# Attention and two feed-forward blocks: scores of the first two pairs made in 32-column strips instead of spread through SBUF

## The chip, the cores and the metric

The kernel runs on one core of one Trainium2 chip. Five engines work from queues of their own and meet at semaphores: PE (matrix products, with its weight loads, PEld), DVE and ACT (vector and activation work), POOL and SP. DMA transfers are issued from the queues of SP, ACT and POOL. The metric is the device time of one execution in microseconds (us), lower is better.

## What is computed

Inputs are q, k, v of shape (2, 12, 448, 64): two batches, twelve heads, 448 rows, 64 columns. Attention mixes the heads twice, before and after softmax:

```
scores = scale * q @ k.T                             # b h i j
scores = einsum('bhij,hg->bgij', scores, w_pre)      # mix heads
attn   = exp(scores - max) / (sum + 1e-9)            # over j
attn   = einsum('bhij,hg->bgij', attn, w_post)       # mix heads
x      = attn @ v                                    # to (896, 768)
x      = ((x @ w_a) * (x @ w_b)) @ w_out             # d_ff 1536
out    = relu(x @ w_in) ** 2 @ w_out2                # d_ff 2048
```

## The kernel before

All matrix products of the two feed-forward blocks follow the attention; they are not touched. Attention goes through the 448 rows of a batch in four tiles of 120, 120, 120 and 88 rows. A tile consists of blocks of ten rows, and two blocks make a **pair**, the unit of the pipeline: six pairs in a full tile, 23 in a batch. `NC` = 6 chunks hold two heads each.

Scores of a tile come from `qk` (L169): for each chunk two matmuls, one per head, on the two halves of the array's rows, with the 120 query rows as output rows and the 448 key columns as moving operand. For the first two tiles they are plain float32; later tiles use a high and a low part of each operand (three products). `qk_copy` (L188) brings the scores to SBUF, the even head by ACT and the odd one by DVE.

The mixing of heads wants another order: for one block, 120 partitions that hold twelve heads times ten rows. So `spread` (L196) sends each head's scores by DMA into `G`, in which partition `13*row + head` holds a score row and the second index counts the blocks. There are two of these, G[0] for tiles zero and two, G[1] for tiles one and three. `premix` (L223) then does the first mixing of a pair: four 64x64 matmuls from G with `wpre_sb`, in the four quadrants of the array, into two banks with the tag `T`.

`softmax` (L625) takes the minima (DVE, L239) and the exponentials (ACT, L246), `weights2` (L252) scales the second mixing's weights by the sums, `post` (L268) does the second mixing (32 small matmul records per pair), `evac` (L285) copies it out. After a tile's pairs, `av` (L301) multiplies with v in three blocks. The main loop (L637) goes through **slots**, one per pair: first mixing of the next pair, second mixing of this one, softmax of the next, and then what a table `mid` gives to the slot (score chunks of a later tile, loads, casts, splits), and `end` (the values). Each engine runs its instructions in the order in which the program writes them.

The start has an order of its own. SP loads the six key chunks, ACT's queue three parts of the first queries, the mixing weights and the queries of tile one. Twelve chunks of scores, six of tile zero and six of tile one, run back to back; tile zero goes to G in three portions (`GS`: blocks 0-1, 2-5 and 6-11), tile one in one. Warming matmuls (`busy`, L339) stand before, between and behind. Portions three of tile zero, the queries of tile two, the spreads of tile one and the load of v follow in `spread_rest` (L369), all behind one another on SP and POOL.

Of the kernel before, what the change touches and what calls it, by code (L numbers as in the profile page):

```python
# [20 lines left out]
KG = 5  # L21
# [43 lines left out]
def attention_moe_kernel(  # L65
    ctx: ExitStack,
    tc: tile.TileContext,
    qT: bass.AP,
    kT: bass.AP,
    v: bass.AP,  # L70
    wpre: bass.AP,
# [16 lines left out]
        return ap.bitcast(F32)  # L88


    wpre_sb = const.tile([128, 128], F32, name="wpre_sb")
    wp = const.tile([128, H, KG], F32, name="wp")

    def single(tag, dtype=F32R):
# [29 lines left out]
    qp = {}  # L124
    qq = {}
    vv = {}
    AVp = {}

    def load_q(b, t, engs=(nc.sync,)):
        x = w_p.tile([128, UW], F32, tag="wc", name="q", bufs=2)  # L130
        n = NC * TILE // len(engs)
        for i, eng in enumerate(engs):
            eng.dma_start(out=x[:, i * n:(i + 1) * n], in_=qT[b, t, :, i * n:(i + 1) * n])
        qq[b, t] = x


    def load_k(b, c):
# [30 lines left out]

    def qk(b, t, c, tags=("qk", "qk")):  # L169
        qk_out()  # L170
        n = ROWS[t]
        p = [ps(tag) for tag in tags]
        if b == 0 and t < 2:
            parts = [(qq[b, t], kk[b, c])]
        else:
            (qh, ql), (kh, kl) = qp[b, t], kp[b, c]
            parts = [(qh, kh), (qh, kl), (ql, kh)]
        for i, (x, y) in enumerate(parts):
            for e in range(2):
                o = 64 * e  # L180
                nc.tensor.matmul(  # L181
                    p[e][0:n, 0:S], x[o:o + 64, c * TILE:c * TILE + n], y[o:o + 64, :],
                    start=(i == 0), stop=(i == len(parts) - 1),
                )
        for e in range(2):
            Sps.append((b, t, 2 * c + e, p[e]))

    def qk_copy(t, h, p, s):  # L188
        n = ROWS[t]
        if h % 2:  # L190
            nc.vector.tensor_copy(s[0:n], p[0:n, 0:S])
        else:
            nc.scalar.copy(s[0:n], p[0:n, 0:S])


    def spread(t, h, s, r0, r1, eng=nc.sync):  # L196
        g = G[t % 2]
        n = r1 - r0
        o = r0 * ROW
        last = ROW - 1 if h == H - 1 else ROW  # L200
        eng.dma_start(out=g[h:PK * (last - 1) + h + 1:PK, r0:r1, :], in_=s[o:o + last * n])
        if last < ROW:
            a = place(last, h)
            eng.dma_start(out=g[a:a + 1, r0:r1, :], in_=s[o + last * n:o + ROW * n])


    def qk_out(which=(0, 1)):
        now = [x for x in Sps if x[2] % 2 in which]
        Sps[:] = [x for x in Sps if x[2] % 2 not in which]
        for b, t, h, p in now:  # L210
            n = ROWS[t]
            s = s_p.tile([TILE, S], F32, tag="s", name="s")
            qk_copy(t, h, p, s)
            full = n // ROW
            spread(t, h, s, 0, full)
            rem = (n - full * ROW) // 2
            for f in range(2 if rem else 0):
                o = full * ROW + f * rem
                a = place(f * KG, h)
                nc.sync.dma_start(out=G[t % 2][a:a + PK * (rem - 1) + 1:PK, full, :], in_=s[o:o + rem])  # L220


    def premix(b, m):  # L223
        t, r, n = PAIRS[m]
        p = [ps("T") for _ in range(2)]
        for g in range(n):
# [6 lines left out]
        Tps[b, m] = p  # L233

    def smin(b, m, f):
        if f == 0:
# [93 lines left out]
    nc.gpsimd.memset(G[0][:, GS[0]:GS[1], :], 0.0)  # L330
    nc.vector.memset(G[0][:, GS[1]:GS[2], :], 0.0)
    nc.gpsimd.dma_start(out=wp, in_=wpost)
    nc.gpsimd.memset(G[0][:, GS[2]:GS[3], :], 0.0)
    nc.vector.memset(G[1][:, 0:6, :], 0.0)
    nc.gpsimd.memset(G[1][:, 6:H, :], 0.0)
    nc.vector.tensor_scalar(wpre_sb, wpre_sb, -0.125, None, ALU.mult)


    def busy(n):  # L339
# [7 lines left out]
    v0 = [sb.tile([128, NJ * DM], F32, tag="v", name="v0", bufs=2) for _ in range(2)]  # L347
    stage1 = [v0[h // 6][0:TILE, (h % 6) * S:(h % 6 + 1) * S] for h in range(H)]
    tags0 = (("qk", "qk"), ("T", "T"), ("post", "post"))
    hw = (nc.gpsimd, nc.sync)  # L350
    for c in range(NC):
        qk(0, 0, c, tags0[c % 3])
        while Sps:
            _, t, h, p = Sps.pop(0)
            qk_copy(t, h, p, stage0[h])
            spread(0, h, stage0[h], GS[0], GS[1], hw[h % 2])
    for h in range(H):
        spread(0, h, stage0[h], GS[1], GS[2], hw[h % 2])
    for c in range(NC):
        qk(0, 1, c, tags0[c % 3])  # L360
        while Sps:
            _, t, h, p = Sps.pop(0)
            qk_copy(t, h, p, stage1[h])
    for c in range(3):
        split_k(0, c)
    busy(4)


    def spread_rest():  # L369
        for c in range(3, NC):  # L370
            split_k(0, c)
        for h in range(H):
            spread(0, h, stage0[h], GS[2], GS[3], hw[h % 2])
        load_q(0, 2)
        for h in range(H):
            spread(1, h, stage1[h], 0, ROWS[1] // ROW, hw[h % 2])
        load_v(0)


    tiles = [(b, t) for b in range(B) for t in range(NTL)]  # L380
# [4 lines left out]
    dve_l, mid, end = {}, {}, {}  # L385

    def at(d, slot, *f):
        d.setdefault(max(slot, 0), []).append(f)

    for ti, (b, t) in enumerate(tiles):  # L390
        s0, sp = base[ti], span[ti]
        if ti + 1 < len(tiles):
            nxt = tiles[ti + 1]
            for c in range(NC if ti else 0):
                at(mid, s0 - 3 + c, qk, *nxt, c)
            if ti + 2 < len(tiles):
                if ti:
                    at(mid, s0 - 2, load_q, *tiles[ti + 2])
                at(mid, s0 + 1, split_q, *tiles[ti + 2])
# [301 lines left out]
def _layout(i):  # L701
# [1 line left out]

    f = np.float32
    q, k, v = i["q"], i["k"], i["v"]
    qT = np.zeros((B, NTL, 128, NC, TILE), f)
    for b, t in np.ndindex(B, NTL):
        n = ROWS[t]
        full = n // ROW
        col = []  # L710
        g = GS if b + t == 0 else (0, full)
        for r0, r1 in zip(g, g[1:]):
            p = np.arange((r1 - r0) * ROW)
            col.append(ROW * (r0 + p % (r1 - r0)) + p // (r1 - r0))
        col = np.concatenate(col + [np.arange(full * ROW, n)]) + OFFS[t]
        qT[b, t, :, :, 0:n] = q[b][:, col, :].reshape(NC, 2, n, D).transpose(1, 3, 0, 2).reshape(128, NC, n)
    kT = k.reshape(B, NC, 2, S, D).transpose(0, 1, 2, 4, 3).reshape(B, NC, 128, S)
    vl = v.reshape(B, H, NJ, JP, D).transpose(0, 3, 2, 1, 4).reshape(B, JP, NJ, DM)
    wpre = np.zeros((128, 128), f)
    wpost = np.zeros((128, H, KG), f)  # L720
    for n in range(ROW):
        for g in range(2):
            o = [place_mixed(g, n, h) for h in range(H)]
            wpre[np.ix_([place(n, h) for h in range(H)], o)] = i["w_pre"]
            wpost[o, :, n % KG] = i["w_post"]

    def units(m):
        kk, n = m.shape
# [6 lines left out]
    return {"qT": qT.reshape(B, NTL, 128, NC * TILE), "kT": kT, "v": vl, "wpre": wpre, "wpost": wpost, "w": wall}  # L735


# [18 lines left out]
```

## Time and profile before

| | |
|---|---|
| median of the runs shown | 759.58 us (758.59 to 760.4, three runs) |
| the profiled execution | 753.42 us, of which its span 751.6 |
| PE busy | 730.6 us, 97% |
| DVE, ACT, POOL busy | 485.4, 310.6, 54.0 us |
| mean granted clock of PE | 0.968 of full |
| read from HBM, written | 62.03 MB, 2.75 MB |

Times in the profile start at the span's beginning. Busy is a share of the whole span; a busy PE can still run at half clock, which the row PEclk tells: 1.00 is 2.4 GHz and 0.50 is 1.2 GHz. The chain of waits is followed back from the last instruction: at each step it names what released the work, or the instruction before it on its engine. A name such as `T<-G` gives output and input by the program's names; `L229` is a line of the program. A float32 matmul leaves two records, so four 64x64 matmuls are x8.

### The profile page before, as it was taken

What the parts mean: (1) busy time and instruction counts of PE and PEld (TensorE: products, weight loads), DVE (VectorE), ACT (ScalarE), POOL (GpSimd) and SP (SyncE); (2) the same over time, 40 slices, a digit from 0 to 9 for tenths busy, and PEclk for the clock granted to TensorE, in tenths of its full rate; (3) what the DMA queues carried; (4) which work ended last, traced back from release to release, by engine and by line L of the source; (5) the groups of instructions that cost most, each with busy time, mean ns of one, the idle gap of its engine ahead of it and who ended that gap; (6) DMA issues with size and microseconds to landing.
All of it is one profiled execution on the core that took longest, in us unless ns stands there. A gap on an engine that the chain in (4) does not pass through costs nothing.

```text
span 751.6 us, 13028 instructions
## 1 busy us (share of the span) xinstructions
PE 730.6 (97%) x5301; PEld 622.3 (83%) x5301; DVE 485.4 (65%) x818; ACT 310.6 (41%) x581; POOL 54.0 (7%) x58
## 2 busy tenths in 40 slices
PE   8799989999989999999999999999999999999997
PEld 3567757676757899999999999999999999999997
DVE  6445666577785477666766765666888888655540
ACT  5244564465562433433343332333555555322220
POOL 8500130000220000000000000000000000000000
PEclk9559999999988999999999999999999999999999
DMA  6773443455230032332332233232323323443310
GB/s 179 171 198 110 126 133 120 129 169 165 76 102 34 2 127 92 119 126 85 126 117 95 92 133 112 85 126 85 126 98 112 124 88 126 150 130 130 127 48 26
DMA packets 26969, 84.89 MB, mean 113 GB/s; under 512 B 3634, under 2 KB 16606, under 8 KB 26686
## 3 DMA queue, kind: packets, MB, share of 16 engines
q1 hardware_dynamic: 24910, 80.65, 33.1%
q0 software_dynamic: 1280, 2.62, 1.7%
q8 instruction: 42, 0.69, 0.4%
q10 hardware_dynamic: 720, 0.80, 0.3%
q14 instruction: 17, 0.14, 0.1%
HBM read 62.03 MB, written 2.75 MB: 86 GB/s over the span
## 4 chain that ended last, share of the span: by engine, by line
PE 91%; DMA 4%; DVE 2%; ACT 1%; issue 1%; SPq 1%; DVEq 0%; ACTq 0%
PE post L279 9%; PE T L507 8%; PE T L508 8%; PE T L506 8%; PE qk L506 6%; PE post L508 6%; PE post L507 6%; PE post L506 5%; PE qk L508 5%; PE qk L507 5%; PE T L229 5%; PE qk L181 4%; PE av L310 4%; PE av L506 3%; PE av L507 3%; PE av L508 3%
## 5 line engine op out<-in xcount | busy, mean ns | idle before, releaser
L279 PEld LDWEIGHTS post<-w,e 64*112 64x112 f32 x1440 | 85.7, 194 | 37.0 <-issue 17.3
L459 ACT CAST wh<-wc 128x768 fp32r<-128x768 f32 x68 | 56.8, 835 | 123.4 <-DVE wc L453 109.9
L246 ACT ACTIVATE e<-T,nb 128x448 f32<-128x448 f32 (+1 forms) x92 | 57.4, 629 | 89.7 <-DVE nb L239 89.6
L279 PE MATMUL post<-w,e 64*112 64x60 f32 x1440 | 92.2, 281 | 2.3 <-DVE w L260 2.3
L464 DVE TENSOR_TENSOR wl<-wc,wh 128x768 fp32r<-128x768 f32 x66 | 63.0, 954 | 48.4 <-ACT wh L459 48.4
L507 PE MATMUL T<-m,wh 128*128 128x448 f32 x213 | 77.9, 366 | 0.2 <-DVE m L482 0.2
L506 PE MATMUL T<-m,wh 128*128 128x448 f32 x213 | 77.9, 366 | 0.0
L508 PE MATMUL T<-m,wl 128*128 128x448 f32 x213 | 77.8, 365 | 0.0
L239 DVE TENSOR_REDUCE nb<-T 128x1 f32<-128x448 f32 (+1 forms) x92 | 53.1, 618 | 30.4 <-PE T L229 30.3
L442 DVE SCALAR_TENSOR_TENSOR wa<-wr,wa 128x768 uint32<-128x768 uint32 x68 | 65.2, 958 | 2.3
L453 DVE SCALAR_TENSOR_TENSOR wc<-wc,wa 128x768 uint32<-128x768 uint32 x68 | 65.1, 958 | 2.2
L229 PE MATMUL T<-G,wpre_sb 64*64 64x448 f32 x360 | 54.1, 616 | 8.1 <-DMA G<-x 3.2
L437 ACT ACTIVATE wc<-wr 128x768 f32<-128x768 f32 x68 | 61.4, 903 | 0.0
L449 DVE TENSOR_SCALAR wc<-wc 128x768 f32<-128x768 f32 x68 | 37.7, 554 | 14.7 <-ACT wc L437 14.7
L508 PE MATMUL post<-m,wl 128*128 128x448 f32 x125 | 45.7, 365 | 0.0
L506 PE MATMUL post<-m,wh 128*128 128x448 f32 x125 | 45.6, 365 | 0.0
L507 PE MATMUL post<-m,wh 128*128 128x448 f32 x125 | 45.6, 365 | 0.0
L296 DVE COPY a<-post 112x480 f32<-112x480 f32 x44 | 30.1, 684 | 20.6 <-PE post L279 18.7
L507 PEld LDWEIGHTS T<-m,wh 128*128 128x128 f32 x213 | 40.0, 188 | 3.7 <-DVE m L482 0.5
L506 PEld LDWEIGHTS T<-m,wh 128*128 128x128 f32 x213 | 40.0, 188 | 3.4 <-ACT m L481 0.3
L508 PEld LDWEIGHTS T<-m,wl 128*128 128x128 f32 x213 | 40.0, 188 | 3.1
L506 PE MATMUL qk<-m,wh 128*128 128x448 f32 x116 | 42.4, 365 | 0.0
(160 smaller groups left out, 1441.1 us busy)
## 6 DMA issues: line engine op xcount, KB each, us to landing
wr<-w SPq DMA_DIRECT2D x68, 768.0 KB
G<-s SPq DMA_DIRECT2D x44, 210.0 KB
G<-s SPq DMA_DIRECT2D x22, 140.0 KB
k<-kT SPq DMA_DIRECT2D x12, 224.0 KB
v<-v SPq DMA_DIRECT2D x2, 1344.0 KB
outT<-ta SPq DMA_DIRECT2D x12, 224.0 KB
q<-qT SPq DMA_DIRECT2D x6, 360.0 KB
G<-v POOLq DMA_DIRECT2D x6, 210.0 KB, 11.9
```

Of the source, the lines that this page charges most:

```text
L229: nc.tensor.matmul(p[f][o:o + 64, 0:S], wpre_sb[i:i + 64, o:o + 64], G[t % 2][i:i + 64, r + g, :], start=True, stop=True, skip_group_check ...
L239: nc.vector.tensor_reduce(out=NB[b, m][0:q, f:f + 1], in_=Tps[b, m][f][0:q, 0:S], op=ALU.min, axis=AX.X)
L246: nc.scalar.activation(out=e[0:q], in_=Tps[b, m][f][0:q, 0:S], func=ACTF.Exp, bias=NB[b, m][0:q, f:f + 1], scale=-1.0, accum_out=Z[b, m][0 ...
L279: nc.tensor.matmul(p[g][0:JP, c:c + k], e[o:o + 64, j * JP:(j + 1) * JP], w2[o:o + 64, f, :], start=True, stop=True,)
L437: nc.scalar.activation(out=st["c"], in_=rd(st["high"]), func=ACTF.Abs, scale=HSC)
L442: nc.vector.scalar_tensor_tensor(out=a, in0=st["high"], scalar=0x80000000, in1=a, op0=ALU.bitwise_and, op1=ALU.bitwise_or)
L453: nc.vector.scalar_tensor_tensor(out=cu, in0=cu, scalar=3, in1=st["a"], op0=ALU.logical_shift_left, op1=ALU.bitwise_or)
L459: nc.scalar.copy(st["hi"], st["c"])
L464: eng.tensor_tensor(out=lo, in0=st["c"], in1=rd(st["hi"]), op=ALU.subtract)
L506: nc.tensor.matmul(p[:, 0:S], hi[:, sl], x[0], start=first, stop=False)
L507: nc.tensor.matmul(p[:, 0:S], hi[:, sl], x[1], start=False, stop=False)
L508: nc.tensor.matmul(p[:, 0:S], lo[:, sl], x[0], start=False, stop=last)
```

## The change

The scores of the first two pairs (`ND` = 2: blocks 0 to 3 of tile zero) no longer go through `spread`. A new input `qD` holds their queries so arranged that `direct` makes a block's scores in the mixing's order: for each block two groups of four matmuls over 128 rows with 32 output columns each, in four strips of columns; a strip adds up two chunks, the halves of `qD` that do not belong to a head being zero. One copy per block brings the 128 partitions to SBUF, and `premix` mixes such a block with 128x64 matmuls and a second copy of the mixing weights. The other eight blocks of tile zero are made by `qk` with 80 instead of 120 rows and go to G in one portion. The scores of tile one are no longer made at the start; two of their chunks stand in each of slots 0 to 2, one ahead of the second mixing and one behind it, and their spreads alternate between POOL and SP. The load of the queries of tile two moves to slot 0, key splits to slots 1 to 3, the load of v to slot 2. Warming matmuls remain only at the very start.

```
-GS = (0, 2, 6, 12)
+ND = 2
+R0 = 2 * ND
+ROWS0 = ROWS[0] - R0 * ROW
+CHUNKS = ((0, 1, 3, 4), (1, 2, 4, 5))
...
+    def load_qd(m, tag, bufs, eng):
+        x = w_p.tile([128, UW], F32, tag=tag, name="qd", bufs=bufs)
+        eng.dma_start(out=x[:, 0:512], in_=qD[m])
+        qd[m] = x
...
-            s = s_p.tile([TILE, S], F32, tag="s", name="s")
-            qk_copy(t, h, p, s)
+            first = b == 0 and t == 1
+            s = stage1(h) if first else s_p.tile([128, S], F32, tag="s", name="s")
+            qk_copy(n, h, p, s)
             full = n // ROW
-            spread(t, h, s, 0, full)
+            spread(t, h, s, 0, full, hw[h % 2] if first else nc.sync)
...
+    def direct(m):
+        for g in range(2):
+            p = ps("T" if g else "av")
+            for i in range(2):
+                for j in range(4):
+                    o = ((g * 2 + i) * 4 + j) * 32
+                    nc.tensor.matmul(
+                        p[32 * j:32 * j + 32, 0:S], qd[m][:, o:o + 32], kk[0, CHUNKS[i][j]],
+                        start=(i == 0), stop=(i == 1), skip_group_check=True,
+                    )
+            x = s_p.tile([128, S], F32, tag="s", name="s")
+            if g:
+                nc.scalar.copy(x, p[:, 0:S])
+            else:
+                nc.vector.tensor_copy(x, p[:, 0:S])
+            Sd[m, g] = x
...
     def premix(b, m):
...
+        if b == 0 and m < ND:
+            for f in range(2):
+                for g in range(2):
+                    nc.tensor.matmul(
+                        p[f][64 * g:64 * g + 64, 0:S], wpre_sb[:, 128 + 64 * f:192 + 64 * f], Sd[m, g],
+                        start=True, stop=True, skip_group_check=True,
+                    )
+            return
...
-    load_q(0, 0, (nc.scalar, nc.scalar, nc.scalar))
+    load_q(0, 0, nc.scalar)
     for c in range(NC):
         load_k(0, c)
+    load_qd(0, "wa", 1, nc.scalar)
     nc.scalar.dma_start(out=wpre_sb, in_=wpre)
-    load_q(0, 1, (nc.scalar,))
+    load_qd(1, "wh", 3, nc.scalar)
+    load_q(0, 1, nc.scalar)
...
+    for c in range(4):
+        first(c)
+        first_out()
+    nc.vector.tensor_scalar(wpre_sb, wpre_sb, -0.125, None, ALU.mult)
+    direct(0)
+    first(4)
+    first_out()
...
+    at(mid, 0, load_q, 0, 2)
+    for c in range(NC):
+        at(mid, 1 + c // 2, split_k, 0, c)
+    at(mid, 2, load_v, 0)
...
+                elif c % 2:
+                    at(mid, c // 2, qk, *nxt, c)
+                else:
+                    at(pre, c // 2, qk, *nxt, c)
+                    at(aft, c // 2, qk_out, (0,))
...
     premix(*plist[0])
-    busy(8)
     softmax(0)
-    spread_rest()
+    direct(1)
     weights2(*plist[0])
+    first(5)
+    first_out()
     for n in range(NS):
...
         qk_out((0,))
+        run(pre, n)
         post(*plist[n])
+        run(aft, n)
```

On PE, before, from the last warming matmuls to the third pair: L229 is the first mixing from G, L279 the second one.

```order
L342 LDWEIGHTS warm
L342 MATMUL av<-warm 1x448
L229 MATMUL T<-G_83,wpre_sb 64x448 x4
L279 MATMUL post<-w_307,e 112x60 x16
L229 MATMUL T<-G_83,wpre_sb 64x448 x4
L279 MATMUL post<-w_346,e 112x60 x16
L229 MATMUL T<-G_83,wpre_sb 64x448 x4
```

The same stretch of PE now: L241 are the direct scores, L193 the score chunks, L260 the mixing from them, L268 the mixing from G, L317 the second mixing.

```order
L241 MATMUL av<-k,qd 32x448 x8
L241 MATMUL T<-k,qd 32x448 x8
L193 MATMUL qk<-k,q 80x448 x2
L260 MATMUL T<-s,wpre_sb 64x448 x4
L241 MATMUL av<-k,qd 32x448 x8
L241 MATMUL T<-k,qd 32x448 x8
L193 MATMUL post<-k,q 80x448 x2
L260 MATMUL T<-s,wpre_sb 64x448 x4
L193 MATMUL qk<-k,q 120x448 x2
L317 MATMUL post<-w_226,e 112x60 x16
L193 MATMUL qk<-k,q 120x448 x2
L268 MATMUL T<-G_83,wpre_sb 64x448 x4
```

Direct scores and score chunks now stand between the mixings, where warming matmuls or nothing stood.

On SP, before, around the queries of tile two (`q<-qT`) and the values (`v<-v`): G_83 is G[0] and G_84 is G[1]; the ones from `v_` are the spreads of tile one.

```order
L201 DMA G_83<-x_2_124 9x6x448
L204 DMA G_83<-x_2_124 1x6x448
L133 DMA q<-qT 128x720
L201 DMA G_84<-v_125 10x12x448 x3
L201 DMA G_84<-v_126 10x12x448 x2
L201 DMA G_84<-v_126 9x12x448
L204 DMA G_84<-v_126 1x12x448
L165 DMA v<-v 112x3072
```

The same place on SP now (odd heads only; `x_` after the queries is tile one too):

```order
L212 DMA G_83<-x_2_125 9x8x448
L215 DMA G_83<-x_2_125 1x8x448
L212 DMA G_84<-v_126 10x12x448
L139 DMA q<-qT 128x720
L212 DMA G_84<-v_126 10x12x448 x2
L212 DMA G_84<-x_0_360 10x12x448
L212 DMA G_84<-x_1_387 10x12x448
L176 DMA v<-v 112x3072
L212 DMA G_84<-x_2_430 9x12x448
L215 DMA G_84<-x_2_430 1x12x448
```

The queries moved ahead of all but one of the spreads of tile one, and the values moved from behind the last head to ahead of it.

## Rows read from the trace of the kernel before

**Rows 1.** The page's clock in 40 slices; digits are tenths of full speed.

```profile
PEclk9559999999988999999999999999999999999999
```

**Rows 2.** The chain of waits, first 64.3 us: start us, us, what.

```profile
...
4.10 3.94 DMA k<-kT
...
9.19 0.75 PE T L181 x4
...
15.20 0.85 PE av L342 x4
16.05 0.98 PE T L229 x8
...
17.68 1.35 ACT e L246 x4
...
19.85 0.98 DVE w L260
...
25.72 12.87 DMA q<-qT
...
46.35 1.70 PE T L229 x8
48.05 3.17 PE post L279 x32
51.23 1.22 PE qk L181 x6
...
58.54 2.43 PE av L310 x32
...
62.61 1.64 PE av L310 x32
...
```

**Rows 3.** Groups by line, 0 to 60 us: count, busy, mean ns, idle before, releasers.

```profile
L229 PE MATMUL T<-G,wpre_sb 64*64 64x448 f32 x56 | 12.9, 856 | 5.8 <-DMA G<-x 3.2 <-DVE w L260 2.3 <-ACT e L246 0.3
```

**Rows 4.** Busy time by stretch: length, engines, clock, DMA share, GB/s.

```profile
20.00:25.00 5.00, 4.14 (x44) 3.36 (x48) 1.99 (x4) 1.80 (x6) 5.00 (x7) 0.73 0.47 127
...
59.50:60.00 0.50, 0.50 (x12) 0.50 (x10) 0.00 (x0) 0.00 (x0) 0.00 (x0) 0.67 0.29 81
```

**Rows 5.** The chain of waits, 64 to 100 us.

```profile
64.25 0.91 PE T L229 x8
65.17 1.72 PE post L279 x32
66.88 0.94 PE qk L181 x6
...
98.44 0.80 SPq L201
```

**Rows 6.** Busy time by stretch, while keys and queries load.

```profile
7.00:8.00 1.00, 0.29 (x2) 0.00 (x0) 1.00 (x3) 0.64 (x2) 0.94 (x2) 1.00 1.04 391
```

**Rows 7.** Transfers, 0 to 80 us: KB each, median us to landing.

```profile
G<-v POOLq DMA_DIRECT2D x6, 210.0 KB, 11.9
...
G<-x POOLq DMA_DIRECT2D x6, 105.0 KB, 5.0
```

**Rows 8.** Groups by line, 0 to 60 us, on ACT.

```profile
L298 ACT COPY a<-post 112x480 f32<-112x480 f32 x6 | 3.9, 643 | 5.1 <-PE post L279 5.1
...
L150 ACT CAST ks<-k 128x448 fp32r<-128x448 f32 x6 | 3.0, 564 | 0.0
...
L193 ACT COPY x<-qk 120x448 f32<-120x448 f32 x2 | 1.1, 532 | 2.8 <-PE qk L181 2.8
```

**Rows 9.** The chain of waits, behind a mixing in batch one.

```profile
234.48 0.40 PE qk L506
234.88 0.20 PE qk L507
```

**Rows 10.** Busy time by stretch, two later ones with gaps.

```profile
108.00:112.00 4.00, 2.17 (x32) 1.65 (x29) 2.42 (x7) 2.40 (x6) 0.20 (x1) 1.00 0.28 75
...
224.00:228.00 4.00, 3.10 (x34) 2.94 (x34) 2.20 (x7) 1.98 (x5) 0.00 (x0) 0.50 0.57 197
```

More of the change, by code (lines that the diff above doesn't have):

```diff
@@ L68, in attention_moe_kernel @@
     qT: bass.AP,
+    qD: bass.AP,
     kT: bass.AP,
@@ L88, in rd @@
         return ap.bitcast(F32)
-    wpre_sb = const.tile([128, 128], F32, name="wpre_sb")
+    wpre_sb = const.tile([128, 256], F32, name="wpre_sb")
     wp = const.tile([128, H, KG], F32, name="wp")
@@ L126, in attention_moe_kernel, with load_q @@
     vv = {}
+    qd = {}
+    Sd = {}
     AVp = {}
-    def load_q(b, t, engs=(nc.sync,)):
+    def load_q(b, t, eng=nc.sync):
         x = w_p.tile([128, UW], F32, tag="wc", name="q", bufs=2)
-        n = NC * TILE // len(engs)
-        for i, eng in enumerate(engs):
-            eng.dma_start(out=x[:, i * n:(i + 1) * n], in_=qT[b, t, :, i * n:(i + 1) * n])
+        n = NC * (ROWS0 if b + t == 0 else TILE)
+        eng.dma_start(out=x[:, 0:n], in_=qT[b, t, :, 0:n])
         qq[b, t] = x
+    def load_qd(m, tag, bufs, eng):
+        x = w_p.tile([128, UW], F32, tag=tag, name="qd", bufs=bufs)
+        eng.dma_start(out=x[:, 0:512], in_=qD[m])
+        qd[m] = x
     def load_k(b, c):
@@ L170, in qk @@
         qk_out()
-        n = ROWS[t]
+        n = ROWS[t] if b + t else ROWS0
+        w = TILE if b + t else ROWS0
         p = [ps(tag) for tag in tags]
@@ L181, in qk @@
                 nc.tensor.matmul(
-                    p[e][0:n, 0:S], x[o:o + 64, c * TILE:c * TILE + n], y[o:o + 64, :],
+                    p[e][0:n, 0:S], x[o:o + 64, c * w:c * w + n], y[o:o + 64, :],
                     start=(i == 0), stop=(i == len(parts) - 1),
@@ L186, in qk, with qk_copy @@
             Sps.append((b, t, 2 * c + e, p[e]))
-    def qk_copy(t, h, p, s):
-        n = ROWS[t]
+    def qk_copy(n, h, p, s):
         if h % 2:
@@ L198, in spread @@
         n = r1 - r0
-        o = r0 * ROW
+        o = 0
         last = ROW - 1 if h == H - 1 else ROW
@@ L225, in premix @@
         p = [ps("T") for _ in range(2)]
+        Tps[b, m] = p
+        if b == 0 and m < ND:
[6 more added lines that the diff above has]
+            return
         for g in range(n):
@@ L324, in attention_moe_kernel @@
     nc.vector.memset(warm, 0.0)
-    load_q(0, 0, (nc.scalar, nc.scalar, nc.scalar))
+    load_q(0, 0, nc.scalar)
     for c in range(NC):
         load_k(0, c)
+    load_qd(0, "wa", 1, nc.scalar)
     nc.scalar.dma_start(out=wpre_sb, in_=wpre)
-    load_q(0, 1, (nc.scalar,))
-    nc.gpsimd.memset(G[0][:, GS[0]:GS[1], :], 0.0)
-    nc.vector.memset(G[0][:, GS[1]:GS[2], :], 0.0)
+    load_qd(1, "wh", 3, nc.scalar)
+    load_q(0, 1, nc.scalar)
+    nc.vector.memset(G[0][:, 4:8, :], 0.0)
+    nc.gpsimd.memset(G[0][:, 8:H, :], 0.0)
     nc.gpsimd.dma_start(out=wp, in_=wpost)
[L333 to L336, printed above, removed]
+    nc.vector.memset(G[0][:, 0:4, :], 0.0)
+    nc.vector.memset(G[1][:, 0:2, :], 0.0)
+    nc.gpsimd.memset(G[1][:, 2:H, :], 0.0)
     def busy(n):
@@ L346, in attention_moe_kernel, with stage1, first, first_out @@
     stage0 = [x[0:TILE, e, :] for x in stages for e in range(2)]
-    v0 = [sb.tile([128, NJ * DM], F32, tag="v", name="v0", bufs=2) for _ in range(2)]
-    stage1 = [v0[h // 6][0:TILE, (h % 6) * S:(h % 6 + 1) * S] for h in range(H)]
-    tags0 = (("qk", "qk"), ("T", "T"), ("post", "post"))
+    v0 = sb.tile([128, NJ * DM], F32, tag="v", name="v0", bufs=2)
+    late = {}
     hw = (nc.gpsimd, nc.sync)
-    for c in range(NC):
-        qk(0, 0, c, tags0[c % 3])
+    def stage1(h):
+        if h < 6:
+            return v0[0:TILE, h * S:(h + 1) * S]
+        if h % 2 == 0:
+            late[h // 2] = xpair(1, h // 2 - 3, F32)
+        return late[h // 2][0:TILE, h % 2, :]
+    def first(c):
+        qk(0, 0, c, ("post", "post") if c % 2 else ("qk", "qk"))
+    def first_out():
         while Sps:
             _, t, h, p = Sps.pop(0)
[L355 to L377, printed above, removed]
+            qk_copy(ROWS0, h, p, stage0[h])
+            spread(0, h, stage0[h], R0, H, hw[h % 2])
+    for c in range(4):
[5 more added lines that the diff above has]
+    first_out()
     tiles = [(b, t) for b in range(B) for t in range(NTL)]
@@ L384, in attention_moe_kernel @@
     NS = len(plist)
-    dve_l, mid, end = {}, {}, {}
+    dve_l, pre, aft, mid, end = {}, {}, {}, {}, {}
     def at(d, slot, *f):
         d.setdefault(max(slot, 0), []).append(f)
+    at(mid, 0, load_q, 0, 2)
+    for c in range(NC):
+        at(mid, 1 + c // 2, split_k, 0, c)
+    at(mid, 2, load_v, 0)
     for ti, (b, t) in enumerate(tiles):
@@ L393, in attention_moe_kernel @@
             nxt = tiles[ti + 1]
-            for c in range(NC if ti else 0):
-                at(mid, s0 - 3 + c, qk, *nxt, c)
+            for c in range(NC):
+                if ti:
+                    at(mid, s0 - 3 + c, qk, *nxt, c)
+                elif c % 2:
[3 more added lines that the diff above has]
+                    at(aft, c // 2, qk_out, (0,))
             if ti + 2 < len(tiles):
@@ L398, in attention_moe_kernel @@
                     at(mid, s0 - 2, load_q, *tiles[ti + 2])
-                at(mid, s0 + 1, split_q, *tiles[ti + 2])
+                at(mid, s0 + (1 if ti else 2), split_q, *tiles[ti + 2])
             if nxt[1] == NTL - 1 and nxt[0] + 1 < B:
@@ L705, in _layout @@
     q, k, v = i["q"], i["k"], i["v"]
-    qT = np.zeros((B, NTL, 128, NC, TILE), f)
+    qT = np.zeros((B, NTL, 128, NC * TILE), f)
     for b, t in np.ndindex(B, NTL):
@@ L709, in _layout @@
         full = n // ROW
[L710 to L716, printed above, removed]
+        r0 = R0 if b + t == 0 else 0
+        p = np.arange((full - r0) * ROW)
+        col = ROW * (r0 + p % (full - r0)) + p // (full - r0)
+        col = np.concatenate([col, np.arange(full * ROW, n)]) + OFFS[t]
+        n = len(col)
+        x = q[b][:, col, :].reshape(NC, 2, n, D).transpose(1, 3, 0, 2).reshape(128, NC, n)
+        if r0:
+            qT[b, t, :, 0:NC * n] = x.reshape(128, NC * n)
+        else:
+            qT[b, t].reshape(128, NC, TILE)[:, :, 0:n] = x
+    qD = np.zeros((ND, 128, 2, 2, 4, 32), f)
+    for m, g, n, h in np.ndindex(ND, 2, ROW, H):
+        a = [x[h // 3] for x in CHUNKS].index(h // 2)
+        o = 64 * (h % 2)
+        qD[m, o:o + 64, g, a, h // 3, ROW * (h % 3) + n] = q[0, h, ROW * (2 * m + g) + n]
     kT = k.reshape(B, NC, 2, S, D).transpose(0, 1, 2, 4, 3).reshape(B, NC, 128, S)
     vl = v.reshape(B, H, NJ, JP, D).transpose(0, 3, 2, 1, 4).reshape(B, JP, NJ, DM)
-    wpre = np.zeros((128, 128), f)
+    wpre = np.zeros((128, 256), f)
     wpost = np.zeros((128, H, KG), f)
@@ L725, in _layout @@
             wpost[o, :, n % KG] = i["w_post"]
+        o = 128 + 64 * (n // KG)
+        for h in range(H):
+            wpre[32 * (h // 3) + ROW * (h % 3) + n, [o + place_mixed(0, n, x) for x in range(H)]] = i["w_pre"][h]
     def units(m):
@@ L734, in _layout @@
     wall = np.concatenate([ab, units(i["moe_w_out"]), units(i["moe2_w_in"]), units(i["moe2_w_out"])], 0).view(np.uint64)
-    return {"qT": qT.reshape(B, NTL, 128, NC * TILE), "kT": kT, "v": vl, "wpre": wpre, "wpost": wpost, "w": wall}
+    return {"qT": qT, "qD": qD.reshape(ND, 128, 512), "kT": kT, "v": vl, "wpre": wpre, "wpost": wpost, "w": wall}
 def kernel(**inputs):
```

1 line of the change is left out of this document (removed).

## The prediction

> **What bounds the kernel now.** I read the clock line first [rows 1]: of 40 slices, the two that cover 19 to 56 us stand at half of the full clock. The chain of waits over the first 64 us says how the kernel gets there [rows 2]. The last key chunks land (8 us), twelve score matmul pairs run at 0.75 us each, four warming matmuls take 0.85 us, the first mixing starts at 16.05. Behind it PE has nothing until softmax is through, then waits for spread scores: the mixing's line shows 2.3 us idle before a release by `w` and 3.2 us before one by the transfers into G [rows 3]. From 25.72 on the chain hangs on one transfer, the queries of tile two (12.87 us): ACT's cast of them stands in front of the next exponentials. The table by stretches dates the clock: mean 0.73 in 20 to 25 (PE busy for 4.14 of 5 us), 0.67 in the half microsecond after 59.5, which is the way back [rows 4], when the first weights-times-values block runs. So some 37 us are at 1.2 GHz. What that costs is read from one pair at either level: mixing 1.70, second mixing 3.17, scores 1.22, together 6.09 us at half [rows 2]; 0.91, 1.72 and 0.94, together 3.57, at full clock [rows 5]. Tile zero ends where the next mixing starts, at 64.25 [rows 5]. From there PE is busy almost throughout, so a gain before 64.25 should stay.
>
> **What the change does, step by step.** I walk PE's new order at full clock.
>
> *To the third chunk.* The warming matmuls stay. The first queries are 240 KB in one transfer instead of 120 KB and two more, so the start may slip by half a microsecond; the fourth chunk still governs, and I start its pair at 8.2 like before.
>
> *Last key chunk.* Before, queries, keys and mixing weights were 2128 KB; now 240+1344+256+128+256 = 2224 KB stand ahead, and the queries of tile one (360 KB) follow in the same flow. At 391 GB/s [rows 6] the extra 96 to 456 KB are 0.2 to 1.2 us. The direct scores need all six chunks; I book 0.3 us of waiting.
>
> *Direct scores, twice.* Sixteen matmuls of 448 columns each in four strips. A score matmul pair of 448 columns takes 0.75 [rows 2]. The trace has no 32-column strip. Nearest are the four 64x64 quadrants of the mixing, all in 0.91 instead of 3.0 one after another [rows 5], and the two 64-column halves of the values block. So four at a time cost 4 x 0.75 + 0.2 = 3.2; two at a time 6.2; none together 12.2. I take 3.2, since the quadrants overlap fully. A change of the array's shape costs 0.2: the first matmul behind a mixing takes 0.40, the next 0.20 [rows 9].
>
> The Trainium skill ("TensorE: Matmul & The Clock Gate", Measured speedup vs the span model) speaks against a full factor of four: it gives 3.07 for four row strips and 2.38 for three column strips. As an estimate from that page, sixteen matmuls of 0.75 at 3.07 are 3.9 us, and the sum would be 1.4 us higher, 747.4. No strip is in this trace, and the quadrants' 0.91 is 3.3 of 4, between the two.
>
> *First two mixings.* They contract 128 rows into 64 columns, two at a time: 2 x 0.75 + 0.2 = 1.7 instead of 0.91.
>
> The Trainium skill ("TensorEngine Tiling (Array Packing)", Key Properties) says that changing the tiling mode drains the array. The trace agrees with 0.2 [rows 9]. The order has some seven more changes, of which four are in the terms above; counting all would add 0.6.
>
> *What goes.* Six of twelve early score pairs (4.5 us), the 0.85 of warming on the chain, the other eight warming matmuls (beside softmax anyway), and of G's tile zero a third of the bytes. The six tile-one pairs come back in slots 0 to 2, six times 0.75.
>
> *PE's line:* 8.2 + 0.75 (fourth pair) + 0.3 + 3.2 (direct) + 0.75 + 1.7 (first mixing) + 3.2 + 0.75 + 1.7 (second mixing) = 20.55. Slot 0: 0.75 + 1.72 + 0.75 = 23.8. Slots 1 and 2, each 0.91 + 0.75 + 1.72 + 0.75 = 4.13: 32.0. Slots 3 to 5, 3.57 each: 42.7. Three blocks of values at 1.64: 47.7.
>
> *Waits on it.* From the end of the first mixing (17.03) to the weights (20.83) softmax of pair 0 took 3.8 us [rows 2]. It now lies beside the second direct scores, a pair and the second mixing, 5.6 us; so the old 2.3 us stall goes. Late next is the third mixing, at about 23.8: it needs head eleven, made at 18.8, copied by 19.5, two issues on SP at 0.80 [rows 5] to about 21. 105 KB took 5.0 us to land in a loaded queue, 210 KB 11.9 [rows 7]; here at most four transfers of 140 KB are under way and I take 2 to 3 us. No wait, but no reserve either. ACT in slots 1 and 2 has two copies (1.06), exponentials 1.35, evacuation 0.64 and two casts 1.13 [rows 2, 8], 4.2 against PE's 4.13, and in slot 2 the queries' cast of 720 columns on top; taken in order, they let score pairs wait for ACT's copies. I book 2.0 us (0 to 4). Tile one's mixing, due at 41 with that, needs heads ten and eleven. Head eleven's spread now stands behind the 1344 KB of values on SP's queue. Values leave at about 32 and take 3.5 us at 391 GB/s [rows 6], 4 to 5 beside other spreads by my estimate; the copy is at 35.5, landing 38 to 42. I book 1.0 (0 to 6.5, the last from a landing of 11.9 us [rows 7]). The queries of tile two now leave before most of tile one's spreads, so the 12.87 us go.
>
> Sum: 47.7 + 2.0 + 1.0 = 50.7 against 64.25: 13.6 us less. On the profiled execution (753.42, span 751.6 and 1.8 around it) that is 739.8. The median of the runs shown is 6.2 above the profiled one; nothing in the rows tells why, and stretches such as 224 to 228 at 0.50 [rows 10] suggest that an execution may have one half-clock stretch more or less. I take the gain off the median: 759.6 - 13.6 = 746.0.
>
> **Rivals.**
>
> *The clock falls all the same (slower).* Place: PE between 8 and 24 us. If it again stands still for 2 us and more (keys late, or head eleven late), the clock falls, and from 20.55 on everything runs at half until the values: 1.5 + 3.17 + 1.5; two slots of 1.70 + 1.5 + 3.17 + 1.5 = 7.87; three of 6.09; values 2.43 + 1.64 + 1.64 [rows 2]. That ends at 66.5, 2.3 later than before: 761.9. It decides as soon as the fall comes before slot 1. For it: six pairs' work at half clock did not bring the clock back before the values [rows 1, 2]. Against: the new order has 12 us of dense 448-column matmuls there, and the gaps of 108 to 112 (busy 2.17 of 4) left the clock at 1.00 [rows 10].
>
> *Strips do not run together.* Two at a time: 6 us more, 752.0. None: 18 us more, 764.0, slower. For it: the trace shows no 32-column strip and no four streams over the same 128 rows. Against: the quadrants.
>
> *Late spreads of tile one.* The values in front of head eleven, and head ten on POOL behind four subtractions of keys and one of queries: 6.5 us at the seventh mixing instead of 1.0, and a clock that falls in it costs one pair at 6.09 and a slower block of values (0.8), 3.3: 754.8. For it: spreads of 210 KB took 11.9. Against: these came behind the rest of tile zero, which is gone.
>
> *Given back later.* Where PE waits on spreads anyway (108 to 112, 1.8 us, and 224 to 228 [rows 10]) an earlier front could wait longer. If SP's queue had been the limit since 48, all would be lost: 759.6. Against: between 64 and 96 PE waits for hardly anything.
>
> **How the numbers follow.** Forecast 62 in 100 (its own range 741 to 751: ACT 0 to 4, seventh mixing, drains, and a later half-clock stretch of some 3 us more or less); two strips at a time 9; late spreads 13; given back 4; clock falls 9; no overlap 3. Faster by more than 0.2% (1.5 us, what a measurement of this kernel tells from no change): 62 + 9 + 13 = 84. Within: 4. Slower: 12. The range of 8 in 10 goes from 739 to 757: it holds the forecast, two strips and late spreads, and leaves out the rest.
>
> **What would show it.** Right: eight direct matmuls of one output in about 1.5 us; the granted clock at 1.00 from 5 to 40; the third mixing near 24, the seventh near 41, tile one's second slot (the end of the values) near 51; from there the pairs at 3.57 as before. Wrong: direct scores of 6 us and more; a clock of 0.5 before 40; the seventh mixing behind a transfer into G by more than 3 us; or a longer stall between 85 and 100 in place of the one from 104 to 112.

## The result: 0.9% faster, half of what was forecast

| | before | after |
|---|---|---|
| median | 759.58 us (756.85 to 760.82, five runs) | 752.65 us (751.95 to 754.36, five runs) |
| profiled execution, span | 753.42, 751.6 | 752.84, 751.1 |
| mean granted clock | 0.968 | 0.975 |

The ratio is 0.9915 [0.989, 0.994]; a second measurement of both in a later session gave 0.9959 [0.9928, 0.9991], 0.4%. The forecast was 746.0, the range 739 to 757: direction and range held, the size did not (6.9 us of 13.6). And the 6.9 us don't lie where I put them, as the sections below show. A few executions of every version take over 1.5% longer than its fastest, ratios leave these out and medians don't, and the first profile under "Both" below is of such a one.

### The profile page after: what moved, and what is told of

The parts are those of the page before. It is cut to its first block, busy times and chain, and to the rows that moved or that the text cites. A ratio compares the mean times of both kernels' runs of the same rounds, so it can differ in the third digit from the quotient of the medians.

```text
span 751.1 us, 13088 instructions
## 1 busy us (share of the span) xinstructions
PE 732.2 (97%) x5353; PEld 619.8 (83%) x5353; DVE 488.3 (65%) x821; ACT 311.0 (41%) x583; POOL 47.6 (6%) x45
## 4 chain that ended last, share of the span: by engine, by line
PE 90%; DMA 4%; DVE 2%; ACT 2%; issue 1%; SPq 1%; POOL 0%; ACTq 0%; DVEq 0%
PE post L317 8%; PE T L552 8%; PE T L553 8%; PE T L551 8%; PE qk L551 6%; PE post L551 6%; PE post L552 6%; PE post L553 6%; PE qk L552 5%; PE qk L553 5%; PE T L268 5%; PE av L348 4%; PE qk L193 4%; PE av L552 3%; PE av L551 3%; PE av L553 3%
## 5 line engine op out<-in xcount | busy, mean ns | idle before, releaser
L317 PEld LDWEIGHTS post<-w,e 64*112 64x112 f32 x1440 | 81.9, 186 | 35.3 <-issue 17.0
L317 PE MATMUL post<-w,e 64*112 64x60 f32 x1440 | 87.6, 272 | 2.9 <-DVE w L298 2.9
L268 PE MATMUL T<-G,wpre_sb 64*64 64x448 f32 x344 | 48.2, 599 | 4.6 <-DMA G<-s 2.2
L553 PE MATMUL qk<-m,wl 128*128 128x448 f32 x116 | 42.4, 365 | 0.0
```

The costliest lines, as they stand in the source:

```text
L268: nc.tensor.matmul(p[f][o:o + 64, 0:S], wpre_sb[i:i + 64, o:o + 64], G[t % 2][i:i + 64, r + g, :], start=True, stop=True, skip_group_check ...
L317: nc.tensor.matmul(p[g][0:JP, c:c + k], e[o:o + 64, j * JP:(j + 1) * JP], w2[o:o + 64, f, :], start=True, stop=True,)
L553: nc.tensor.matmul(p[:, 0:S], lo[:, sl], x[0], start=False, stop=last)
```

## The profile after

The chain of waits of the changed kernel (start us, us, what), tile zero first, then the end of tile one, and one mixing of tile two:

```profile
5.29 6.03 DMA k<-kT
...
14.72 1.65 PE T L260 x8
16.38 1.64 PE av L241 x16
18.02 1.50 PE T L241 x16
...
20.43 1.65 PE T L260 x8
...
25.52 1.10 PE T L268 x8
...
37.39 1.60 POOL ql L171
...
39.05 8.27 DMA G<-x
...
47.73 1.89 PE T L268 x8
49.61 3.17 PE post L317 x32
...
60.20 0.91 PE T L268 x8
...
105.18 2.75 DMA G<-s
...
108.02 2.17 PE T L268 x8
...
121.20 0.91 PE T L268 x8
...
137.28 0.91 PE T L268 x8
```

The front of tile zero stands where [rows 2] had the early scores, softmax and the 12.87 us for the queries. Direct scores (L241) and the new mixing (L260) run back to back, and neither the old 2.3 us stall [rows 3] nor the queries are on the chain. Third mixing: 25.52 (forecast 23.8). From there it slips: the chain goes through POOL's subtraction of the queries (`ql`) and, behind it, the issue of head ten's spread, which takes 8.27 us, to the seventh mixing at 47.73 (forecast 41). Tile zero ends at 60.20, against 64.25 [rows 5] and 50.7 forecast. Tile one ends at 121.20; in the first profile of before its end is at 121.25. So, against that profile, the 4.05 us won by the end of tile zero are gone again by the end of tile one.

Busy time by stretch (length, PE, weight loads, DVE, ACT, POOL, clock, DMA share, GB/s):

```profile
20.00:24.00 4.00, 4.00 (x40) 2.08 (x38) 2.49 (x4) 1.58 (x4) 0.57 (x1) 1.00 0.24 65
...
32.00:36.00 4.00, 4.00 (x56) 2.48 (x54) 2.20 (x7) 3.65 (x9) 2.59 (x4) 1.00 0.67 194
36.00:40.00 4.00, 2.88 (x37) 1.99 (x38) 3.88 (x7) 3.51 (x10) 3.98 (x5) 0.90 0.95 223
40.00:44.00 4.00, 3.38 (x28) 1.94 (x25) 3.63 (x4) 1.76 (x5) 1.88 (x2) 0.50 0.87 229
44.00:48.00 4.00, 2.92 (x26) 2.30 (x28) 1.18 (x4) 1.18 (x3) 0.00 (x0) 0.50 0.89 220
...
56.00:60.00 4.00, 4.00 (x79) 3.97 (x76) 0.81 (x2) 0.00 (x0) 0.00 (x0) 0.96 0.21 58
...
104.00:108.00 4.00, 1.72 (x20) 1.04 (x17) 1.80 (x6) 2.07 (x6) 0.00 (x0) 0.94 0.28 76
108.00:112.00 4.00, 3.98 (x28) 2.48 (x30) 1.69 (x3) 1.06 (x3) 0.00 (x0) 0.50 0.52 138
```

The clock is full to 36, not only to 20 as in [rows 4]. In 36 to 40 four things meet: PE busy 2.88 of 4, DVE 3.88, POOL 3.98, and the DMA engines 0.95 of their time. The clock falls to half (1.2 GHz) and stays there until the values. It falls again at 104 to 108, where PE is busy for 1.72 of 4 us and waits for spread scores; POOL is idle there and the DMA engines are at 0.28.

What PE waited for from 36 to 60 (engine, line, releaser: us in all, times, longest):

```profile
PE qk L193 <- POOL ql L171: 1.1, 1, 1.1
PE T L268 <- DMA G<-x: 1.1, 1, 1.1
PE post L317 <- DVE w L298: 0.6, 1, 0.6
```

Three waits of about a microsecond or less, one of each kind: POOL, a transfer, DVE. They are 2.8 us in all; the rest of the loss is work at half clock. What made POOL and DVE late is in their timelines (start us, us, engine, line, operation):

```profile
29.74 0.15 DVE L296 TENSOR_SCALAR z<-z 128x2 f32<-128x2 f32 x1
...
30.13 0.28 DVE L298 TENSOR_TENSOR w<-wp,z 128x120 f32<-128x120 f32 x1
...
37.98 1.15 DVE L296 TENSOR_SCALAR z<-z 128x2 f32<-128x2 f32 x1
...
39.36 2.67 DVE L298 TENSOR_TENSOR w<-wp,z 128x120 f32<-128x120 f32 x1
...
37.39 1.71 POOL L171 TENSOR_TENSOR ql<-q,qh 128x720 fp32r<-128x720 f32 x1
39.05 0.59 POOL L212 DMA_DIRECT2D G<-x  x1
39.66 2.23 POOL L162 TENSOR_TENSOR ks<-k,ks 128x448 fp32r<-128x448 f32 x2
```

The same two DVE instructions take 0.15 and 0.28 with POOL quiet (its next subtraction starts at 30.44), 1.15 and 2.67 beside POOL's subtractions, and each ends just after a subtraction ends (39.13 after 39.10, 42.03 after 41.89). The second mixing of that pair waits for `w`. (`w` lies beside two subtractions in a row and ends with the second; why it didn't get in between them isn't shown.)

The Trainium skill ("SBUF — State Buffer", Who interferes with whom) says that DVE and GpSimd share one pair of SBUF ports and that holding it is an exclusive lock; a DVE instruction with two SBUF inputs contends with a GpSimd instruction that reads SBUF. The trace agrees for `w`, which has two inputs in SBUF: 2.67 instead of 0.28. `z` has one, so that sentence doesn't cover it; here it is long all the same. I could have seen it: in [rows 2] `w` took 0.98 at 19.85, beside POOL's subtractions of keys in the trace of before:

```profile
16.28 6.61 POOL L151 TENSOR_TENSOR ks<-k,ks 128x448 fp32r<-128x448 f32 x6 [0.99 <-ACT ks L150]
```

## The experiments

Four theories were tried. POOL: its subtractions, moved into slots 1 to 3, hold up DVE and with it PE, and the clock falls. Bytes: spreads and values in slots 2 to 5 are too much for the transfer engines. Queue: only the place of the load of v among SP's issues is wrong. Give-back (G in the expectations): what tile zero wins is lost at 104 because of the load of batch one's v. Ratios are against before in the same session, whose medians were 757.9, 755.42 and 758.75.

**Before once more.** No edit.

> The kernel before, unchanged, to see what its profiled execution hides. Its profile of 753.42 us ran 6.2 us under the median, and its clock stayed full through the stall of 104 to 112 us. Theory A (the stall near 104 drops the clock in the usual execution, as it does in the changed kernel): a second profile shows 0.50 from about 108 to 117 and a time near 759.6, with a mean clock near 0.957. Theory B (the usual execution is slower at its start): the end of tile zero's values comes near 70 instead of 64.25, the clock after 100 is 1.00. Ratio 1.000 either way.

Measured: 759.59, ratio 1.0037 [0.9995, 1.0078]. Its profile (span 757.4) ends tile zero at 60.49, not at 64.25, so B is out. It falls to half clock from about 103 to 117, as A had it, and once more from about 141 to 147, which neither theory had.

**v behind head eleven** (queue).

```
-    at(mid, 2, load_v, 0)
+    at(mid, 3, load_v, 0)
```

> The changed kernel with the load of v behind tile one's last head instead of ahead of it (slot 3 for slot 2). Theory L (the late spreads of heads ten and eleven set the seventh mixing, because 1344 KB of values share the engines with them): head ten lands some 4 us after its issue instead of 8.3, the seventh mixing starts at 44 to 46 instead of 47.73, time 1 to 3.5 us under the changed kernel. Theory C (the clock's fall at 39.6, behind the wait for the queries' low part, sets it; PE at half clock gets to the seventh mixing only at 46.65): at most 1.1 us.

Measured: 755.11, 0.9955 [0.9927, 0.9983]. Tile zero ends at 60.85, the clock falls at the same place (0.90 in 36 to 40), and `w` takes 2.65. The seventh mixing still stands 3.0 us for a transfer, to 48.97. The queue alone is refuted.

**Query split later** (POOL).

```
-                at(mid, s0 + (1 if ti else 2), split_q, *tiles[ti + 2])
+                at(mid if ti else pre, s0 + (1 if ti else 3), split_q, *tiles[ti + 2])
```

> The changed kernel with the split of tile two's queries behind the copy of head ten, so that POOL issues head ten's spread ahead of the queries' subtraction. Theory L: issue at 36.8 instead of 39.05, landing near 45 instead of 47.3, the seventh mixing at 46 or so, time 1 to 2 us under the changed kernel. Theory C: the wait for the subtraction stays or grows by 0.3 us, the clock falls at the same place, time within 1 us of the changed kernel.

Measured: 752.23, 0.9908 [0.9876, 0.994]. Head ten's spread leaves in time and the seventh mixing (46.75) doesn't wait for G, but now `z` takes 3.89 beside POOL and the clock falls all the same; it comes back earlier, and tile zero ends at 56.38.

**The low part of these queries on DVE instead of POOL** (POOL).

```
-        nc.gpsimd.tensor_tensor(out=lo[:, 0:n], in0=x[:, 0:n], in1=rd(hi)[:, 0:n], op=ALU.subtract)
+        eng = nc.vector if b + t == 2 and b == 0 else nc.gpsimd
+        eng.tensor_tensor(out=lo[:, 0:n], in0=x[:, 0:n], in1=rd(hi)[:, 0:n], op=ALU.subtract)
```

> The changed kernel with the low part of tile two's queries subtracted by DVE instead of POOL, which takes away PE's wait of 1.1 us at 38 and lets POOL issue head ten's spread 1.7 us earlier. Theory C (that wait drops the clock): 1.00 through 41, the values end near 56, time 4 us under the changed kernel. Theory L: the clock falls anyway in the longer wait for the spreads (PE gets to the seventh mixing at 42, the spreads land at 45 or later), the values end at 58 to 60, time 0 to 2 us under the changed kernel.

Measured: 754.57, 0.995 [0.9921, 0.9979]; tile zero ends at 61.49. Of POOL's load only the keys are left there, and `w` is back at 0.28; but DVE's own subtraction of 720 columns takes 1.89 us from 37.35 (one of 768 takes 0.96 later in the kernel), with POOL's keys ending at 38.48 in the midst of it, and the minima of the next pair wait behind it. Moving the work to the other engine of the two doesn't help.

**One subtraction per slot** (POOL): keys in slots 1 to 6, queries in slot 1.

```
-        at(mid, 1 + c // 2, split_k, 0, c)
+        at(mid, 1 + c, split_k, 0, c)
...
-                at(mid, s0 + (1 if ti else 2), split_q, *tiles[ti + 2])
+                at(mid, s0 + (1 if ti else 1), split_q, *tiles[ti + 2])
```

> The changed kernel with the split of tile two's queries in slot 1 instead of 2 and one key split per slot (1 to 6) instead of two (1 to 3). Theory P (POOL's subtractions in slots 2 and 3 set the loss: PE waits 1.1 us for the queries' low part, DVE's small operations on z take 2.6 to 3.9 us beside them instead of 0.15 to 0.3, and these gaps drop the clock): the wait at 38 goes, z and w of pair four take under 0.5 each, slot 3 lasts 3.6 to 4.0 instead of 5.2, PE reaches the seventh mixing at 41 to 43. Under P alone the values end at 52 to 55. Theory L (the spreads of tile one come late by themselves): the seventh mixing stays at 46 to 47 behind a transfer into G, the clock falls there, the values end at 57 to 59.

Measured: 756.25, 1.0015 [0.9987, 1.0044], no gain. The chain of waits:

```profile
39.50 0.91 PE T L268 x8
40.41 1.76 PE post L317 x32
42.18 8.67 DMA G<-s
50.85 1.88 PE T L268 x8
```

At 39.50 PE is still at full clock, and `z` and `w` take 0.15 and 0.28 throughout, so POOL's part is cured; then PE stands for 7.8 us for transfers, and tile zero ends at 64.22. The row names the transfer that landed last, a spread of tile two's scores (`s`), which this mixing doesn't read; of those that it reads, head ten's, issued at 37.35, took 11.6 us. The transfers are left.

**The same, with v behind head eleven** (POOL and queue).

> The same with the load of v behind tile one's last head. Theory P: no difference to the run with the splits alone, values end at 52 to 55. Theory L: the spreads land 2 to 4 us earlier, the seventh mixing at 42 to 44, values end at 51 to 54, 3 to 5 us ahead of the run with the splits alone. If tile one's values then wait for v (landing after 48), theory L is right and v has taken its place.

Measured: 750.93, 0.9915 [0.9878, 0.9951]. The chain:

```profile
40.36 9.55 DMA v<-v
...
50.05 3.47 PE av L348 x32
```

The seventh mixing comes at 43.25 at full clock; now the load of v takes 9.55 us, the values wait, and tile zero ends at 57.95. The wait went from one end of the queue to the other, which speaks for the bytes.

**Batch one's v four slots later, in after and in before** (give-back).

```
-            at(mid, s0 + sp, load_v, b + 1)
+            at(mid, s0 + sp + 4, load_v, b + 1)
```

> The changed kernel with the load of batch one's v in slot 16 instead of 12, behind the spreads of tile three. Theory G (given back: what tile zero gained is lost in the stall of 101 to 108, in which PE waits for spreads that share the engines with 1344 KB of v, and the clock falls after it): the waits for G<-s of 4.55, 1.82 and 2.75 us shrink to under 2 in all, the clock stays at 1.00 through 120, the values of tile one end at 113 to 116 instead of 121.1, time 4 to 7 us under the changed kernel. Rival S (the stall is made by SP's issues, three for each head of tile three, 2.1 us a head): the stall and the fall stay, time within 1.5 us of the changed kernel.

> The kernel before with the same move of batch one's v. Theory G: the stall of 104 to 112 goes in it too, its values of tile one end at 115 to 117 instead of 121.2, the time falls by 4 to 7 us and spreads less from run to run. Rival S: within 1.5 us of the kernel before.

Measured: 747.91, 0.9905 [0.9874, 0.9935], and 752.83, 0.993 [0.989, 0.9969]. With the edit in after, tile zero is the same (60.48), and at 104:

```profile
104.00:108.00 4.00, 3.19 (x34) 1.76 (x32) 2.02 (x6) 1.68 (x6) 0.00 (x0) 1.00 0.24 62
108.00:112.00 4.00, 3.97 (x67) 3.46 (x66) 2.37 (x7) 2.31 (x6) 0.00 (x0) 1.00 0.88 252
```

PE is busy 3.19 instead of 1.72, the clock stays full, and tile one ends at 115.29 instead of 121.20. So 5.5 to 5.9 us lie there (121.20 and 120.80 in the two profiles of after), in a load that the change doesn't touch. The profiles bear it out: of the thirteen without this edit twelve fall to half clock somewhere between 98 and 123 (the first of before is the exception), of the three with it none. In the time it is less sure: 0.9905 lies close to after's own 0.9915 and 0.9959 from other sessions. In before the edit ends tile one at 112.3, but the median falls by 2.6 us only (752.83 against 755.42), less than the 4 to 7 expected, and spreads no less (745.41 to 763.96).

**After once more**, and **v early**: the load of v right behind the starting spreads of head nine, when the engines have room (0.24 busy in 20 to 24): the bytes are spread, POOL is left as it is.

```
     first_out()
+    load_v(0)
...
-    at(mid, 2, load_v, 0)
```

> The changed kernel, unchanged, for a second profile and its time beside the versions of this call. Theories P and L say the same: the wait for the queries' low part near 38, DVE's w of 2.7 us beside POOL's subtractions, the clock at 0.50 from about 40 to 56, the values of tile zero ending at 59 to 61; the stall after 101 with a fall to 0.50 until the values of tile one, which end at 121. Time 751 to 754.

> The changed kernel with the load of v issued on SP behind head nine's spread, at about 15 us, where the transfers stand at 65 to 146 GB/s, instead of in slot 2, where they stand at 220. Theory D (transfers bound slots 2 to 5: some 5.3 MB between 24 and 47 us at about 225 GB/s): with 1.4 MB out of the way the last spreads land by 42 to 43, the seventh mixing no longer waits for G. Theory P (POOL's subtractions): the wait at 38, the slow w and the fall of the clock stay, PE reaches the seventh mixing at 46.6, so only 1 us is won, values end near 59. If D alone were right: clock full to 50, values end near 53.

Measured: after 754.96, 0.9959 [0.9928, 0.9991], the same picture (tile zero ends at 60.23, `w` 2.66, falls at about 41 and 107). With v early 750.48, 0.9917 [0.9865, 0.9969]:

```profile
36.00:40.00 4.00, 3.09 (x44) 2.03 (x36) 3.50 (x6) 4.00 (x11) 3.74 (x3) 1.00 0.39 119
40.00:44.00 4.00, 2.13 (x18) 1.17 (x20) 3.93 (x5) 1.26 (x3) 2.93 (x4) 0.89 0.47 131
44.00:48.00 4.00, 4.00 (x38) 3.37 (x40) 1.88 (x6) 2.00 (x6) 0.00 (x0) 0.50 0.48 141
```

The engines' share is down from 0.95 to 0.39 and the seventh mixing waits for no transfer, yet DVE is at 3.93, PE at 2.13, and the clock falls: POOL alone is enough. `w` is at 2.67 again, so the full transfer engines aren't what makes it long. Tile zero ends at 57.44. In the time v early is not clear of after: the two intervals overlap.

**Both**, and **both with batch one's v later** (one subtraction per slot and v early together; the second also with batch one's v four slots later).

> Both: v early, and the splits spread over the slots. Theories D and P together say that nothing of the loss in slots 3 to 5 is left: the seventh mixing at 43 (as in the run with v behind the last head), no wait for v, clock 1.00 from 5 to 50, values of tile zero end at 51 to 52, 8 to 9 us before the changed kernel. The stall after 93 follows at the same distance, so the time is 742 to 747. If the clock falls all the same before 45, neither theory is enough.

> The same with batch one's v in slot 16 instead of 12. Theory G (the later stall gives back what was won by dropping the clock): values of tile zero at 51 to 52, values of tile one end at 106 to 108 without a fall between, time 735 to 742, ahead of all kernels so far. If it equals the run without this move, the later stall does not matter.

Measured: 747.68, 0.9857 [0.9806, 0.9907], and 741.88 (738.32 to 744.9), 0.9809 [0.9759, 0.9858], the lowest of all. Both intervals lie below that of after in the same session (0.9928 to 0.9991); between the two they overlap. In the first's profile the first 96 us are at full clock. Its chain:

```profile
36.05 0.91 PE T L268 x8
36.97 1.71 PE post L317 x32
38.68 0.94 PE qk L193 x6
39.62 0.91 PE T L268 x8
...
43.19 1.04 PE T L268 x8
...
52.04 0.91 PE T L268 x8
```

Pairs at 3.57, nothing else on the chain. The clock row of the second, tenths of full speed in 40 slices (one is 18.4 us):

```profile
PEclk9999999999979999999999999999999999999999
```

Tile zero ends at 51.50, tile one at about 106.3, and one fall is left, at about 206 to 216. It has the same sign: at 201.14 and 202.69 `z` and `w` take 1.31 and 0.97, beside POOL's subtractions from 199.52 to 203.52, and PE stands for 2.27 us until `w` is done:

```profile
200.00:204.00 4.00, 1.53 (x11) 0.43 (x12) 3.09 (x5) 2.10 (x6) 3.52 (x3) 1.00 0.23 65
204.00:208.00 4.00, 4.00 (x50) 2.56 (x50) 2.99 (x8) 2.74 (x6) 0.00 (x0) 0.71 0.12 35
```

Before has it as well: 1.31 and 0.97 at 216 to 219, ahead of the half clock of 224 to 228 in [rows 10]. No kernel was run without these subtractions.

The ends of tile zero in us, one profile each (after: two):

| | v in slot 2 | v early |
|---|---|---|
| subtractions in slots 1 to 3 | 60.20, 60.23 | 57.44 |
| one per slot | 64.22 | 52.04, 51.50 |

Either cure alone leaves a stall that takes the clock; together they give 8 to 9 us. A single profile is thin where before's own end of tile zero differs by 8.4 us (below). What carries the table is that each chain names another stall, that after's end repeats (60.48 with batch one's v later), and that the times of both together are clear of after's.

**Before, two more executions.** What was open: whether the first profile of before is its usual one.

> A third profile of the kernel before. Its first one ended tile zero's values at 64.25 and tile one's at 121.2, its second at 60.5 and 121.2, and the second then lost 6 us more behind a transfer of 5.57 us at 133. Theory V (before, gaps that stand at the edge of dropping the clock decide from execution to execution; only some of the median's 3 to 7 us were won in the first 64 us): this one ends tile zero's values at 60 to 65, has a fall after 100 or one near 140 or both, and its time follows their number. Theory W (the first profile is the usual start): tile zero at 64 to 64.5 and the fall after 100.

> A fourth, the same. Under theory V the sum of half-clock time after 100 us explains most of the difference in time between the four profiles; under theory W the start is alike in all but the second.

Measured: 754.16 and 754.1. The clock row of the first of them, to be laid beside [rows 1]:

```profile
PEclk9679989899978999999999999999999999999999
```

| | end of tile zero | end of tile one | from there to the span's end |
|---|---|---|---|
| before, four profiles | 64.25, 60.49, 58.31, 55.84 | 121.25, 121.26, 116.50, 116.25 | 630.4, 636.1, 635.8, 636.1 |
| after, two profiles | 60.20, 60.23 | 121.20, 120.80 | 629.9, 630.0 |

The profile that I predicted from had the latest end of tile zero of the four. Against the other three, after is level or 2 to 4 us late there, and level or up to 5 us late at the end of tile one. What it wins lies behind: three of four profiles of before fall to half clock between 132 and 148, as does before with batch one's v later; none of the eleven of after and of its variants does. The chain of before's second profile, there:

```profile
133.29 5.57 DMA G<-s
...
138.90 1.27 PE T L229 x8
```

SP issues ten spreads in a row there, from 110.72 to 134.06 in this profile and from 110.45 to 133.99 in the first of after. In this one the tenth, issued at about 133.3 as in after, lands 5.57 us after its issue and the mixing waits; in after the mixing at 137.28 (in the first chain of after above) waits for nothing. Why it lands sooner isn't settled; no kernel was run that changes this alone.

## Why the prediction was right or wrong

- *Direct scores, right.* Sixteen matmuls took 1.64 + 1.50 = 3.14 us, forecast 3.2: 16 x 0.75 / 3.14 is 3.8 of 4. The Trainium skill's factor of 3.07 for four row strips ("TensorE: Matmul & The Clock Gate", Measured speedup vs the span model) would have given 3.9 us, an estimate; here the measurement decides. The rivals "strips do not run together" are out.
- *First two mixings, right*: 1.65, forecast 1.7.
- *Last key chunk, too small.* Booked 0.3; the first direct scores start at 11.37 instead of 9.25, and the third mixing is 1.7 late. The last chunk took 6.03 us to land, with the DMA engines at 0.94 from 8 to 12 us; which of the new loads made it late was not run.
- *What goes, right.* The stall of 2.3 and the queries' 12.87 are off the chain, and the clock holds through the start; the slower rival (a fall between 8 and 24) didn't come.
- *Waits on it: the step that failed.* I booked 2.0 us for ACT and 1.0 for late spreads. From the third mixing to the end of tile zero the sum had 50.7 - 23.8 = 26.9 us, of which 3.0 waits; measured 60.2 - 25.5 = 34.7, 7.8 more. Slots 1 to 3 took 14.3, 0.4 over what the booked waits allow; slot 4 took 7.94 and slot 5 with the values 12.47, 3.4 and 4.0 too long, both mostly at half clock. The length of the waits was not what failed: from the third mixing on PE stands idle for 3.3 us, against 3.0 booked. The sum kept the full clock through them. By the stretches some 17 us ran at half clock; PE was busy for 15.4 of them, work of 7.7 at full clock, and that is nearly all of the 7.8 (an estimate: at full clock PE would have come to the spreads earlier and waited longer, as the run with one subtraction per slot did). Three things were not in the step. The subtractions moved into slots 1 to 3 were counted as queue entries on POOL, never as a hold on DVE (`w` 2.67 for 0.28). Transfers were priced one by one: 360 + 1344 KB of loads and tile one's spreads, some 4.9 MB between 24 and 48 by the GB/s of the stretches, and from 36 on at 220 to 229 GB/s with shares of 0.87 to 0.95, not at the 391 of the key loads [rows 6]. And a fall of the clock, which I let in only before slot 1 or at the seventh mixing at 3.3 us, came at about 39 (0.90 in 36 to 40) and stayed for 17 us. The table of four shows the first two to be separate; without them tile zero ends at 51.5 to 52.0, where the sum had 50.7. So the rest of the sum holds.
- *Late spreads of tile one* was the rival nearest to what came: seventh mixing at 47.5 (47.73), 754.8 (752.65). Its place, head ten behind the subtractions on POOL, is what the chain shows. It had 13 in 100.
- *Given back later* had the place (104 to 108) and the wrong reason: not SP's queue, but batch one's v beside the spreads, and the clock that falls in the stall. I gave it 4 in 100, since in the profile of before that stall [rows 10] left the clock at full; in three of four it didn't.
- *The base.* 64.25 was one draw of a number that goes from 55.84 to 64.25. With the sum's own 50.7 the gain at tile zero against the other three would have been 5 to 10 us, not 13.6. By the profiles the gain in the median doesn't come from the front at all: at the end of tile one after is level with two of before's profiles and 4 to 5 us behind the other two. It comes from the fall at 132 to 148 that is gone, 5.4 to 6.2 us in three of four. I had not foreseen that fall, and why it is gone isn't settled; that the time lies in the range is luck.

## What to carry to other kernels

Where a change moves elementwise work between engines, look at what the neighbour engine runs in the same microseconds: a DVE instruction that is longer than its twins, beside a POOL subtraction, is the sign. Sum the bytes that a stretch must move and divide by the rate of the same kind of transfer, before pricing any transfer by itself. And where a kernel lives near stalls that take the clock, take the base from several profiled executions, and cure all causes of a stall together, since any one of them is enough for the fall.

## What the hardware did that I had not expected

- The same program falls to half clock in different places from one execution to the next: four profiles of before, of spans 751.6 to 757.4, end tile zero at four different times.
- In the changed kernel a load of 1344 KB in slot 12 cost 5.5 to 5.9 us in stalls and half clock by the end of tile one; four slots later the clock stayed full there.
- A stretch with PE busy 2.17 of 4 us left the clock full in one profile [rows 10]; with 2.88 of 4, the changed kernel's 36 to 40 did not, and with 2.87 in its second profile the fall came only after 40.
